# First FFN products by tiles of 128 tokens, in a fused sliding-window attention and SwiGLU kernel

## The chip, the cores and the metric

The kernel runs on one core of a Trainium2 chip. The time is device microseconds for one execution; eight runs of the kernel before had a median of 359.01 us (357.98 to 361.54). The profile comes from one execution, which took 359.05 us.

## What is computed

Attention over eight batches of 576 tokens, eight heads of 64, each token seeing itself and the 127 before it, with a bias by distance that differs by head. Its output, as 4608 tokens of 512, goes through a SwiGLU block:

```python
scores = scale * np.matmul(q, k.transpose(0, 1, 3, 2))
bias = slopes[:, None, None] * (-np.abs(rel).astype(np.float32))[None, :, :]
mask = (rel >= 0) & (rel < window)
scores = np.where(mask, scores + bias[None], -1000000000.0)
...
g = x @ w_gate
silu = g * (1.0 / (1.0 + np.exp(-g)))
val = x @ w_val
return (silu * val @ w_out).astype(np.float32)
```

The sizes of the block are 512 (model) and 1536 (hidden). Inputs and output are fp32; the kernel loads them converted to fp16.

## The kernel before

**Attention.** Batches are taken two at a time: four pairs (s), each with nine units (p), one for each tile of 128 query tokens (the ninth joins the last 64 tokens of both batches). A tile of 128 tokens of q, k or v is called by its rank, nine to a pair. For each unit, `scores` (line 226) multiplies k by q into score banks of PSUM (pool `ps_a`, tag "a", four banks, line 129); ACT takes the exponential (line 259), and DVE multiplies with the table that holds bias and mask (line 263). `weighted` (line 294) multiplies these weights with v, whose 65th column of ones gives the sums, and DVE divides (lines 316, 317). `x_transposed` (line 327) turns the result and ACT copies it to `xT` (line 341), the FFN's input. Each instruction at line 254 needs q and k transposed: up to rank 8 by PE (line 201, copy at 204 or 206), from rank 9 on by DMA transposes on SP's queue (line 222). The units up to FIRST = 4 use the gv banks (pool `ps_f`, three banks, line 128) for weighted sums; `REPEAT` (line 27) says how often PE makes a transpose at the start.

**FFN.** Nine blocks of 512 tokens. For each of twelve hidden slices m, `gate_val` (line 369) makes the gate product pg and the value product pv (line 363, `wide`, four matmuls each), ACT a tanh (374), DVE the gate sum uu (376) and the product hT (380). For block 0, `wide` may be called early for some of the columns; it keeps the bank in `early`, and a later call completes it. `OTHER` names the products that then use a score bank. Block 0's output projection is at line 393. The blocks from 1 to 7 use Strassen's scheme for the output projection: `sums` (line 443) makes sums of hT on DVE, and `strassen` (line 456) seven products of six matmuls (line 472) for each of two column tiles, with evacuations to ACT and DVE (lines 476 to 499) between. They are spread over the next block's half-steps (a gate or value product of one slice): `AT` (line 507) lists the half-steps after which one of the 14 products comes.

**Order.** Each engine works in program order. The first stage, `first_tiles` (line 566), and the first eight steps of the FFN are written out by hand for PE, DVE and ACT (`manual_schedule`, lines 659 to 667). After it, attention steps are drawn in at a rate that depends on the FFN step (lines 668 to 683), and a scheduler orders the instructions of each engine by a cost model when the kernel is built. Loads of q, k, v and weights are issued on POOL's queue (lines 168, 174, 609, 634); each waits until the transfer eight issues earlier has landed. A wait in a queue holds everything behind it. The first loads, up to w_out, are listed in lines 612 to 634.

Of the kernel before, what the change touches and what calls it, by code (L numbers as in the profile page):

```python
# [16 lines left out]
P = 128  # L17
# [6 lines left out]
ENGINES = {"all": None, "compute": {ET.PE, ET.DVE, ET.Activation}, "pe": {ET.PE}}  # L24
WARM = 7
IDLE = {("k", 0): 0, ("q", 0): 2}
REPEAT = {("q", 1): 4, ("k", 1): 4, ("q", 2): 3}
FIRST = 4
LEAD = 6
PRE = 0  # L30
# [4 lines left out]
def slot(h):  # L35

    return 4 * (h // 4) + 2 * (h % 2) + (h % 4) // 2
# [9 lines left out]
def kernel(  # L47
# [10 lines left out]
    nc = tc.nc  # L58
# [21 lines left out]
    idm = consts.tile([P, P], FP16, name="idm")  # L80
    nc.scalar.dma_start(idm, idm_d.ap())

    idm2 = consts.tile([P, P], FP16, name="idm2")
# [5 lines left out]
    def first_masks():  # L89
        nc.vector.tensor_copy(idf, idm)  # L90
        for h in sorted(range(H), key=slot):
            nc.scalar.activation(reg[:, slot(h), :], dist, AF.Exp, scale=-(2.0 ** (-8.0 * (h + 1) / H)))
# [5 lines left out]
    idle = kT[:, NK - 1].rearrange("p j t -> p (j t)")  # L98
# [66 lines left out]
    def load_v(rank):  # L165
        va[rank] = va_all[rank % NV]
        for (p0, p1), src in source(v, rank):
            nc.gpsimd.dma_start(va[rank][p0:p1, :, 0:D], src)  # L168
# [8 lines left out]
    def load(rank):  # L177
        load_qk(rank)
        load_v(rank)

    def transposed(name, rank):
# [16 lines left out]

        for _ in range(REPEAT.get((name, rank), 2) if rank < FIRST else 1):
            for j in range(4):  # L200
# [25 lines left out]
    def scores(i):  # L226

        s, p = units[i]
        def combined(n):
            return scores_128(s, (3, 7, 8)[n], 8, (s, "c", n), msk[n])  # L230

        def together(one, two):
            return [one[0] + two[0]] + one[1:] + two[1:]

        if p == 8:
            return together(combined(1), combined(2))
        if p == 7:
            return together(scores_128(s, p, p, (s, p), reg[:, :, 0:P]), combined(0))
        if p == 3:
            return scores_128(s, p, p, (s, p), reg[:, :, 0:P])  # L240
        ks = (9 * s + p) % NK
        banks = []
        e = epool.tile([P, H, 256], FP16, name="ex", tag="ex", bufs=4)
        ex[(s, p)] = e

        def products():
            for q4 in range(2):
                two = [ps_a.tile([P, 2, 256], FP32, name="ps", tag="a") for _ in range(2)]
                banks.append(two)
                for j in range(2):  # L250
                    pair = 2 * q4 + j
                    for par in range(2):
                        rows = slice(64 * par, 64 * par + 64)
                        nc.tensor.matmul(two[par][:, j, :], kT[rows, ks, pair, :],  # L254
                                         qT[rows, p:p + 2, pair, :], start=(j == 0), stop=(j == 1))

        def act(q4, par):
            o = 4 * q4 + 2 * par
            nc.scalar.activation(e[:, o:o + 2, :], banks[q4][par], AF.Exp, scale=scale)  # L259

        def mul(q4):
            o = slice(4 * q4, 4 * q4 + 4)
            nc.vector.tensor_mul(e[:, o, :], e[:, o, :], reg[:, o, :])  # L263

        return [[products], [lambda: act(0, 0)], [lambda: act(0, 1), lambda: mul(0)],
                [lambda: act(1, 0)], [lambda: act(1, 1), lambda: mul(1)]]
# [27 lines left out]
    def weighted(i):  # L294

        s, p = units[i]
        x = xpool.tile([P, H, D], FP16, name="x", tag="x")
        xs[i] = x
        for half in range(2):
            pool, tag = (ps_f, "gv") if i < FIRST else (ps_a, "a")  # L300
            av = pool.tile([P, 4, D + 1], FP32, name="av", tag=tag)
            todo = []
            for j in range(4):
                h = 4 * half + j
                if p == 8:
                    for n, kt in enumerate((3, 7, 8)):
                        todo.append((j, ex[(s, "c", n)][:, slot(h), :], va[9 * s + kt][:, h, :]))
                else:
                    if p not in (0, 4):
                        todo.append((j, ex[(s, p - 1)][:, slot(h), 128:256],  # L310
                                     va[9 * s + p - 1][:, h, :]))
                    todo.append((j, ex[(s, p)][:, slot(h), 0:128], va[9 * s + p][:, h, :]))
            for n, (j, w, val) in enumerate(todo):
                nc.tensor.matmul(av[:, j, :], w, val, start=(n == 0), stop=(n == len(todo) - 1))  # L314
            rec = xpool.tile([P, 4, 1], FP32, name="rec", tag="rec", bufs=4)
            nc.vector.reciprocal(rec, av[:, :, D:D + 1])
            nc.vector.tensor_mul(x[:, 4 * half:4 * half + 4, :], av[:, :, 0:D],  # L317
                                 rec.broadcast_to([P, 4, D]))
# [31 lines left out]
    hT = {}  # L350

    early = {}
    OTHER = {(0, 1, "v"), (0, 2, "g"), (0, 2, "v")}

    def wide(n, m, which, c1=512):

        w, ms = wg_sb if which == "g" else wv_sb, slice(m * P, (m + 1) * P)
        ps, c0 = early.pop((n, m, which), (None, 0))
        if ps is None:
            pool, tag = (ps_a, "a") if (n, m, which) in OTHER else (ps_f, "gv")  # L360
            ps = pool.tile([P, 512], FP32, name="p" + which, tag=tag)
        for kb in range(NKB):
            nc.tensor.matmul(ps[:, c0:c1], w[:, kb, ms], xT[n][:, kb, c0:c1],  # L363
                             start=(kb == 0 and c0 == 0), stop=(kb == NKB - 1 and c1 == 512))
        if c1 < 512:
            early[(n, m, which)] = (ps, c1)
        return ps
# [136 lines left out]

    AT = {*range(2, 9), *range(10, 17)}

    def ffn():

        for n in range(NBLK):
# [6 lines left out]
            for m in range(NMB):  # L518
                for half, _ in enumerate(gate_val(n, m)):
                    yield 1.0  # L520
                    if n > 1 and 2 * m + half in AT:
                        next(parts)
# [25 lines left out]
    def transposes_to(n):  # L548
        nonlocal done_t
        while done_t < n:  # L550
            transpose(done_t)
            done_t += 1
# [7 lines left out]
    def run(steps):  # L560
        for fs in steps:
            for f in fs:
                f()
            yield

    def first_tiles():

        first_masks()
        transposes_to(need[0] + 1)
        for n, _ in enumerate(run(scores(0))):  # L570
            if n == 2:
                transposes_to(need[1])
        for i in range(FIRST):
            if i + 1 < FIRST:
                for n, _ in enumerate(run(scores(i + 1))):
                    if n == 0 and i + 2 < FIRST:
                        transposes_to(need[i + 2])
            weighted(i)
            if i > 0:
                x_transposed(i - 1)  # L580

        for m, which in ((0, "g"), (0, "v"), (1, "g")):
            wide(0, m, which, 384)
        x_transposed(FIRST - 1)
        for m, which in ((1, "v"), (2, "g"), (2, "v")):
            wide(0, m, which, 384)

    def attention():

# [17 lines left out]
    def load_w(c0, c1):  # L607
        for src, dst in ((wg2, wg_sb), (wv2, wv_sb)):
            nc.gpsimd.dma_start(dst[:, :, c0:c1], src[:, :, c0:c1])
# [8 lines left out]
    load_qk(3, "k")  # L618
    load_v(2)
    load_v(3)  # L620
    load_w(0, 128)
    load_w(128, 512)
    load(4)
    load_qk(5, "q")
    load_w(512, 1024)
# [29 lines left out]
    def everything():  # L655
        nonlocal done
        base = 0
        busy(WARM)
        with tc.manual_schedule(engines=ENGINES[MANUAL]):
            first_tiles()  # L660
            done = FIRST
            steps = progress(ffn())
            while (at := next(steps)) < ALONE:
                if at == 4.0:
                    make_masks()
                if at == 6.0:
                    nc.scalar.copy(idm2, idm)
        for step in steps:

            b1 = 24 + 3 * PRE  # L670

            lead = LEAD if done < X_DMA_FROM - 2 else LEAD + 4
            blk = (0 if step + LEAD < b1 else 1 if step + LEAD < 60
                   else min(NBLK - 1, 2 + int((step + lead - 60) // 34.5)))
            if step < b1:

                target = base + max(0, step - ALONE) + max(0, step - 16) * (32 - b1 + ALONE) / (b1 - 16)
            elif step < 60:
                target = base + 32 + SECOND * 8 * (step - b1) / (60 - b1)
            else:  # L680
                target = base + 32 + SECOND * 8 + (step - 60) * RATE * 8 / 34.5
            while (n_att < target or done < ready[blk]) and att_step():
                pass

    everything()


# [28 lines left out]
```

## Time and profile before

| | |
|---|---|
| median of eight runs | 359.01 us |
| profiled execution | 359.05 us |
| its span, first to last instruction | 357.3 us |
| PE busy | 340.1 us, 95% |
| DVE busy | 271.0 us, 76% |
| DMA, 2 to 57 us | 169 to 181 GB/s |
| first FFN product starts | 21.43 us |
| first tanh starts | 25.97 us |
| first score of unit 9 starts | 60.67 us |
| projection of the last block starts | 343.24 us |

An idle time counts for the end only where the chain of work that ended last passes through it. The timeline gives for each instruction the idle time of its engine before it and what ended that time. The ends of matmuls are modelled, so a start is more reliable than an end.

### The profile page before, as it was taken

To read this page: it belongs to the slowest core of one execution; us is meant where nothing else is said; L and a number is where in the kernel's file an instruction comes from. 1 tells how busy PE (TensorE), PEld (TensorE's weight loads), DVE (VectorE), ACT (ScalarE), POOL (GpSimd) and SP (SyncE) were. 2 spreads that over 40 slices of the span, in tenths; PEclk is the share of its full clock that TensorE was granted. 3 is DMA by queue.
4 is the path that set the end of the run, shared out by engine and by line. 5 is a ranking of instruction groups with operands and counts; after the bars stand their busy time and mean duration, and the time that the engine had idled before them with its cause. 6 is when DMAs were issued, how large, how long until landed. Compare 5 with 4: busy or idle time off the path is not lost.

```text
span 357.3 us, 7133 instructions
## 1 busy us (share of the span) xinstructions
PE 340.1 (95%) x2701; PEld 193.8 (54%) x2701; DVE 271.0 (76%) x594; ACT 177.7 (50%) x351; POOL 107.0 (30%) x132
## 2 busy tenths in 40 slices
PE   7788997999999999999999999999999999999995
PEld 4554443444556645565466655564665566456543
DVE  4748974997987699768987998789877955975540
ACT  4837684455655455556565454555454323333321
POOL 8954652565827372844500001000000000000000
PEclk9999999999999999999999999999999999999999
DMA  9999999999999999999993213202021201101104
GB/s 151 172 186 186 167 175 99 141 134 149 161 142 147 154 155 185 178 153 163 171 106 89 42 65 32 87 18 75 15 76 29 75 4 57 60 2 60 60 17 103
DMA packets 159939, 37.87 MB, mean 106 GB/s; under 512 B 150432, under 2 KB 155424, under 8 KB 159904
## 3 DMA queue, kind: packets, MB, share of 16 engines
q0 software_dynamic: 116224, 18.62, 79.2%
q1 hardware_dynamic: 43232, 18.49, 28.5%
q8 instruction: 21, 0.34, 0.4%
q10 hardware_dynamic: 448, 0.30, 0.3%
q14 instruction: 14, 0.11, 0.1%
HBM read 37.91 MB, written 9.44 MB: 133 GB/s over the span
## 4 chain that ended last, share of the span: by engine, by line
PE 70%; DMA 12%; DVE 8%; POOL 4%; ACT 3%; issue 3%; ACTq 0%; POOLq 0%; SPq 0%; DVEq 0%
PE pg L363 21%; PE pv L363 21%; PE po L472 15%; DMA wv_sb<-in_moe_w_val_dram 6%; PE av L314 3%; PE ps L254 3%; DMA wo_sb<-in_moe_w_out_dram 3%; DMA qn<-in_q_dram 2%; PE po L393 2%; PE p L472 2%; DVE hT L380 2%; DVE uu L376 2%; POOL va L168 1%; ACT exc L286 1%; PE px L340 1%
## 5 line engine op out<-in xcount | busy, mean ns | idle before, releaser
L374 ACT ACTIVATE tt<-pg 128x512 f16<-128x512 f32 x108 | 64.8, 602 | 109.5 <-PE pg L363 103.5
L363 PE MATMUL pg<-xT,wg_sb 128*128 128x512 f16 (+2 forms) x444 | 115.4, 374 | 1.0 <-ACT xT L341 0.7
L363 PE MATMUL pv<-xT,wv_sb 128*128 128x512 f16 (+2 forms) x444 | 113.1, 373 | 1.2 <-DVE uu L376 1.2
L376 DVE SCALAR_TENSOR_TENSOR uu<-tt,pg 128x512 f16<-128x512 f16 x107 | 73.0, 683 | 37.9 <-ACT tt L374 37.3
L380 DVE TENSOR_TENSOR hT<-uu,pv 128x512 f16<-128x512 f16 x108 | 73.8, 683 | 6.0 <-PE pv L363 2.6
L363 PEld LDWEIGHTS <-wg_sb 128*128 128x128 f16 x444 | 41.6, 98 | 38.0 <-issue 3.5
L363 PEld LDWEIGHTS <-wv_sb 128*128 128x128 f16 x444 | 41.2, 98 | 38.5 <-issue 4.9
L259 ACT ACTIVATE ex<-ps 128x512 f16<-128x512 f32 x96 | 50.0, 608 | 9.7 <-PE ps L254 9.6
L168 POOL DMA_DIRECT2D va<-in_v_dram x40 | 34.2, 866 | 43.7 <-PE av L314 34.8
L174 POOL DMA_DIRECT2D qn<-in_q_dram x39 | 33.6, 866 | 35.7 <-DMA qT<-qn 18.4
L174 POOL DMA_DIRECT2D kn<-in_k_dram x39 | 33.3, 858 | 27.3 <-DMA kT<-kn 20.1
L472 PEld LDWEIGHTS <-hT 128*128 128x128 f16 x336 | 32.2, 98 | 14.9 <-issue 1.0
L263 DVE TENSOR_TENSOR ex<-ex,m_reg 128x1024 f16<-128x1024 f16 x48 | 32.8, 686 | 8.4 <-ACT ex L259 8.3
L472 PEld LDWEIGHTS <-S 128*128 128x128 f16 x252 | 23.9, 98 | 12.6 <-issue 4.1
L317 DVE TENSOR_TENSOR x<-av,rec 128x256 f16<-128x256 f32 x72 | 28.6, 420 | 0.4
L286 ACT ACTIVATE exc<-psc 128x512 f16<-128x512 f32 x40 | 21.0, 603 | 5.7 <-PE psc L282 5.7
L472 PE MATMUL po<-T,hT 128*128 128x256 f16 x168 | 22.9, 272 | 0.1
L472 PE MATMUL po<-T,S 128*128 128x256 f16 x168 | 22.9, 273 | 0.0
L314 PE MATMUL av<-va,ex 128*128 128x65 f16 x384 | 20.7, 193 | 2.2 <-DVE x L317 1.3
L314 PEld LDWEIGHTS <-ex 128*128 128x128 f16 x384 | 18.1, 97 | 6.3 <-DVE x L317 2.0
L254 PE MATMUL ps<-qT,kT 64*128 64x256 f16 x192 | 18.0, 272 | 3.6 <-DMA qT<-qn 2.0
L393 PE MATMUL po<-wo_sb,hT 128*128 128x512 f16 x84 | 19.7, 379 | 0.0
(72 smaller groups left out, 279.5 us busy)
## 6 DMA issues: line engine op xcount, KB each, us to landing
out_dram<-osb SPq DMA_DIRECT2D x32, 256.0 KB, 3.2
va<-in_v_dram POOLq DMA_DIRECT2D x32, 128.0 KB, 8.6
qn<-in_q_dram POOLq DMA_DIRECT2D x31, 128.0 KB, 7.4
kn<-in_k_dram POOLq DMA_DIRECT2D x31, 128.0 KB, 7.8
wo_sb<-in_moe_w_out_dram POOLq DMA_DIRECT2D x2, 768.0 KB, 9.6
wg_sb<-in_moe_w_gate_dram POOLq DMA_DIRECT2D x2, 512.0 KB, 10.6
wv_sb<-in_moe_w_val_dram POOLq DMA_DIRECT2D x2, 512.0 KB, 12.3
out_dram<-osb SPq DMA_DIRECT2D x6, 128.0 KB, 2.3
```

The lines of the kernel that those rows point to most:

```text
L168: nc.gpsimd.dma_start(va[rank][p0:p1, :, 0:D], src)
L174: nc.gpsimd.dma_start(t_[p0:p1], src)
L254: nc.tensor.matmul(two[par][:, j, :], kT[rows, ks, pair, :], qT[rows, p:p + 2, pair, :], start=(j == 0), stop=(j == 1))
L259: nc.scalar.activation(e[:, o:o + 2, :], banks[q4][par], AF.Exp, scale=scale)
L263: nc.vector.tensor_mul(e[:, o, :], e[:, o, :], reg[:, o, :])
L314: nc.tensor.matmul(av[:, j, :], w, val, start=(n == 0), stop=(n == len(todo) - 1))
L317: nc.vector.tensor_mul(x[:, 4 * half:4 * half + 4, :], av[:, :, 0:D], rec.broadcast_to([P, 4, D]))
L363: nc.tensor.matmul(ps[:, c0:c1], w[:, kb, ms], xT[n][:, kb, c0:c1], start=(kb == 0 and c0 == 0), stop=(kb == NKB - 1 and c1 == 512))
L374: nc.scalar.activation(tt, pg, AF.Tanh, scale=0.5)
L376: nc.vector.scalar_tensor_tensor(out=uu, in0=tt, scalar=one if (n, m) == PIN else 1.0, in1=pg, op0=ALU.add, op1=ALU.mult)
L380: nc.vector.tensor_mul(hT[n][:, m, :], uu, pv)
L472: nc.tensor.matmul(dst, a[:, m, cols], b[:, m, :], start=(start and m == 0), stop=(m == HM - 1), skip_group_check=True)
```

## The change

In the first stage, the products of block 0 for the slices m = 0 and 1 (gate and value) are begun as soon as the first tile of 128 tokens of xT is there, and continued tile by tile; those for m = 2 begin with two tiles. They were made for three tiles at once before, after the last of the weighted sums. The four products for m = 0 and 1 now lie in score banks. In the weighted sums of units 1 to 3, two products of zeros come first in each bank, which the real ones then overwrite. The counts of repeated transposes change, and q of rank 2 is transposed a little sooner. The first 512 columns of the gate and value weights are loaded as 256 and 256 instead of 128 and 384. The second copy of the identity is made at step 2 instead of 6, the masks at step 5 instead of 4. In the steps of the Strassen products, 4 and 10 are left out instead of 9, and 17 is added: from the third product of a block on, each comes half a step later.

```diff
-REPEAT = {("q", 1): 4, ("k", 1): 4, ("q", 2): 3}
+REPEAT = {("q", 1): 4, ("k", 1): 2, ("q", 2): 4}
...
             av = pool.tile([P, 4, D + 1], FP32, name="av", tag=tag)
+            if 0 < i < FIRST:
+
+                for _ in range(2):
+                    nc.tensor.matmul(av.rearrange("p j d -> p (j d)")[:, 0:256], idle[:, 0:P],
+                                     idle[:, 0:256], start=True, stop=True)
...
-    OTHER = {(0, 1, "v"), (0, 2, "g"), (0, 2, "v")}
+    OTHER = {(0, 0, "g"), (0, 0, "v"), (0, 1, "g"), (0, 1, "v")}
...
-    AT = {*range(2, 9), *range(10, 17)}
+    AT = {2, 3, *range(5, 10), *range(11, 18)}
...
+    def begin(n, tiles):
+
+        for m, which in ((0, "g"), (0, "v"), (1, "g"), (1, "v"), (2, "g"), (2, "v"))[:n]:
+            if early.get((0, m, which), (None, 0))[1] < tiles * P:
+                wide(0, m, which, tiles * P)
+
     def first_tiles():
 
         first_masks()
         transposes_to(need[0] + 1)
         for n, _ in enumerate(run(scores(0))):
-            if n == 2:
+            if n == 0:
                 transposes_to(need[1])
...
             weighted(i)
+
+            if i >= 2:
+                begin(4, i - 1)
             if i > 0:
                 x_transposed(i - 1)
-
-        for m, which in ((0, "g"), (0, "v"), (1, "g")):
-            wide(0, m, which, 384)
+        begin(6, 2)
+        begin(4, 3)
         x_transposed(FIRST - 1)
-        for m, which in ((1, "v"), (2, "g"), (2, "v")):
-            wide(0, m, which, 384)
+        begin(6, 3)
...
-    load_w(0, 128)
-    load_w(128, 512)
+    load_w(0, 256)
+    load_w(256, 512)
...
-                if at == 4.0:
+                if at == 2.0:
+                    nc.scalar.copy(idm2, idm)
+                if at == 5.0:
                     make_masks()
-                if at == 6.0:
-                    nc.scalar.copy(idm2, idm)
```

## The prediction

> **What bounds the kernel now.** I read the page first, then the chain that ended last in order of time, then the waits and the timeline of PE, then DMA by stretches. The page says that PE is the bound overall:
>
> ```profile
> span 357.3 us, 7133 instructions
> PE 340.1 (95%) x2701; PEld 193.8 (54%) x2701; DVE 271.0 (76%) x594; ACT 177.7 (50%) x351; POOL 107.0 (30%) x132
> PE 70%; DMA 12%; DVE 8%; POOL 4%; ACT 3%; issue 3%; ACTq 0%; POOLq 0%; SPq 0%; DVEq 0%
> ```
>
> 95% is an average over two regimes. The chain that ended last, in order of time, separates them (start, length, what):
>
> ```profile
> 12.34 8.00 DMA wv_sb<-in_moe_w_val_dram
> ...
> 22.55 13.07 DMA wv_sb<-in_moe_w_val_dram
> ...
> 36.84 9.43 DMA wo_sb<-in_moe_w_out_dram
> ...
> 47.43 8.74 DMA qn<-in_q_dram
> ...
> 56.25 4.29 DMA qT<-qn
> 60.54 0.14 issue
> 60.67 0.27 PE ps L254
> 60.94 0.97 PE pg L363 x4
> ```
>
> Up to 60.67 us no PE instruction is on the chain: it consists of loads, one handing over to the next on the POOL queue, then the transpose of q of rank 10 on SP's queue, which releases the first product of the first scores of batches 2 and 3 (unit 9). From there on it is PE nearly throughout. The change works before 27 us, inside the first regime. PE's timeline shows where it meets the loads (start, length, instruction, idle time before it and its releaser):
>
> ```profile
> 21.43 0.81 PE L363 MATMUL pg<-xT,wg_sb 128*128 128x384 f16 x4 [0.67 <-ACT xT L341]
> 37.56 0.40 PE L201 MATMUL pt<-idm,qn 128*128 128x128 f16 x4 [0.21 <-DMA qn<-in_q_dram]
> 60.67 0.27 PE L254 MATMUL ps<-qT,kT 64*128 64x256 f16 x1 [2.03 <-DMA qT<-qn]
> ```
>
> These are two gates. At 37.56 PE waits for the load of q of rank 6, issued at 24.57 and landed 13.0 us later, at 37.57. At 60.67 it waits for the rank-10 transpose. Are the loads limited by DMA, or by PE freeing buffers? By stretches (length, busy time of PE, PEld, DVE, ACT, POOL, then granted clock, DMA share, GB/s):
>
> ```profile
> 2.00:20.00 18.00, 13.94 (x175) 9.44 (x174) 11.55 (x37) 11.84 (x25) 17.08 (x21) 1.00 2.11 179
> 20.00:40.00 20.00, 17.72 (x140) 9.84 (x141) 13.26 (x25) 11.64 (x23) 11.35 (x15) 1.00 1.84 181
> 40.00:57.00 17.00, 15.93 (x169) 8.62 (x168) 14.39 (x35) 12.75 (x25) 8.19 (x10) 1.00 1.97 169
> 60.67:343.30 282.63, 279.72 (x2154) 159.47 (x2155) 228.47 (x493) 137.73 (x273) 68.90 (x83) 1.00 0.96 95
> ```
>
> DMA moves 169 to 181 GB/s from 2 to 57 us without a hole: in stretches of one microsecond, about 155 for q, k, v and 205 for weights, and only 40 to 41 us is lower (119). POOL's issues wait for the landing of the transfer eight issues earlier. So the time at which a load lands is a matter of the bytes ahead of it, not of PE. After 60.67, PE's idle time is 282.63 - 279.72 = 2.9 us: that is all that any later rearrangement could win.
>
> [...] the transposes that SP issued at 53.52, 54.87 and 56.25 land at 59.6, 60.1 and 60.5, when the loads issued on POOL up to 50 us have drained. [...] Here four 384-column products take 0.65 us and four 128-column ones 0.22, against 0.65 / 3 = 0.217. [...] The 2.03 us stall here leaves the clock at 1.00.
>
> **The change part by part.**
>
> *Transposes at the start.* k of rank 1 is transposed twice instead of four times: 8 fewer at 0.056 = 0.45 us. q of rank 2 four times instead of three: 4 x 0.056 = 0.22 more. Its copy (DVE, 0.42) now stands before both multiplications (0.69 each) of the first scores, instead of between them. Before, the copy ran at 11.24, behind a multiplication that had waited 1.01 us for ACT, and the second scores at 11.71 waited 1.24 us for it. The new order frees PE by some 1.0 us, of which the score banks that ACT still holds (its exponentials would end near 11.3) leave about 0.8.
>
> *Idle products.* 12 of 256 columns; six of that width start to start take 0.655 us (the groups of line 472), so 12 x 0.109 = 1.31 us. They lie between 12 and 21 us, where PE idles 0.41 + 0.26 + 0.77 + 0.28 + 0.16 + 0.67 = 2.55 us. If that cover were gone they would cost 1.31.
>
> *First products by tiles of 128.* Same columns (six products, four k-blocks, 512 columns each); 40 more instructions, at 0.22 per four no dearer. What moves is the time: 4 x 0.22 = 0.88 us of tile 0 ahead of the second x transpose, 0.88 of tile 1 ahead of the third. Together 1.76 us leave the run that now begins at 21.43, but filler and idle time compete for the same 2.55 us, and DVE, which runs without a hole from 12.9 to 21.5, sets when the last x comes. With the 0.8 from above I estimate that the six products end 1.5 us earlier than 26.9, and the first tanh (25.97 now) as much.
>
> *Banks.* Four of the six now sit in the four score banks, the pair of m=2 in two of three gv banks. The product of v for m=3 therefore waits for the third gate sum (two tanh-sum-product rounds later on DVE, 0.69 each); now it is at 28.20. DVE starts its queue of sums (idle 5.09 us until 26.60 now) 1.5 us earlier, so up to the first gate the head start stays about 1.5 us.
>
> *Weights in slices of 256 and 256.* Same bytes, same four issues. The four landed by 20.34 at 191 to 204 GB/s, later weights at 203 to 209, so at most 5% of the 0.5 MB in narrow slices, 0.13 us. I take 0.
>
> *Masks and second identity moved by a step.* 4 x 0.62 + 0.30 us of ACT, covered by its 2.30 us wait before 33.93. Without cover they would delay one tanh by up to 0.6. I take 0.
>
> *What the shift does to the queues.* In the program as built, POOL issues k and q of rank 8 ahead of both w_out halves instead of between them, and v of rank 9 ahead of k of rank 9. The set ahead of q of rank 10 is the same, so it lands at 56.2 again. k of rank 9 lands behind v: 54.3 becomes about 55.3 (one load of 128 KB in fp16 lands 0.7 to 1.2 us after another here). SP takes its transposes in order at 1.2 us each: 55.3 + 1.2 = 56.5 instead of 56.25 for rank 10. All end in one bunch behind the loads, so between 0 and 0.4 us later; I take +0.2.
>
> *Half a step later.* Seven blocks with two groups of seven products each; from the third product of a block on, each comes one half-step later. The waits of PE after 60 us:
>
> ```profile
> PE po L472 <- DVE osb L476: 1.2, 3, 0.4
> ```
>
> Three of 14 times the sixth product waits for the evacuation that follows the fifth, because a tanh and a gate sum (0.60 + 0.68) stand before it on DVE when the fifth comes after a gate product. The shift puts the fifth after a value product, and the seventh in the same position relative to the sixth's evacuation. Bounds: -1.2 if the waits vanish, 14 x 0.4 - 1.2 = +4.4 if every group gets one. I take 0, the waits changing place.
>
> *Sum.* PE passes the same work between the gates: leaving out filler, the same columns of products stand ahead of unit 9's scores in both programs. So the 1.5 us are waited out: 0.21 us of wait at 37.56 becomes about 1.7, and PE goes on at 37.57 as now. At unit 9 it arrives at 58.6 or, with DVE's backlog drained, up to 1 us earlier, and waits until 60.7 + 0.2. After that PE does what it does now. 357.3 + 0.2 = 357.5 of span, plus the 1.75 us by which the profiled execution (359.05) exceeds its span: 359.2. The median of the runs, 359.01, is within 0.04 of that execution.
>
> **Rivals.** *The head start reaches the end (faster).* For it, the gates must open earlier: q of rank 10 no longer waits in POOL's queue behind the landing of the first w_out half (46.28) and could be issued 1.4 us sooner, near 46.0. If it lands as much earlier, with all its transposes, unit 9 starts near 59.3; with the three waits gone too: 359.05 - 1.4 - 1.2 = 356.5; the first alone gives 357.6. Against it: DMA is full, and an earlier issue only stands longer in the queue.
>
> *Rank 9's k blocks SP (slower).* One mechanism: v ahead of k holds k's transpose, and rank 10's behind it in order. It decides (over 0.5%) once rank 10's transpose ends 1.8 us late, that is issued at 58.1, k landing at 56.9 or later, 2.6 us after now; one load costs about 1. At that point 360.9.
>
> *The half-step makes waits (slower).* At half of the 14 groups, 7 x 0.4 - 1.2 = +1.6: 360.7; at all of them 363.4. For it: the fifth-sixth pattern does return one product later. Against it: PE has other work between the two.
>
> *Half clock.* [...] I expect 2 to 3.
>
> **How the numbers follow.** Absorbed, 0.60, its own range 358.1 to 360.3. Head start reaches the end, 0.20. Rank 9's k on SP 0.06, half-step waits 0.10, half clock 0.04. A measurement of this kernel can tell about 0.5%, 1.8 us, from no change. Nearly all of the first case lies within it, as do small forms of the others: same 0.62, faster 0.20, slower 0.18. Leaving one in ten at each end, inside the faster case's 356.5 and the slower cases' 361 to 363, gives 357.0 to 361.3.
>
> **What would show it.** Right: first tanh near 24.5; the wait for the rank-6 q grown from 0.21 to 1 to 2 us with the product still at 37.5; unit 9's first score at 60.5 to 61.1 with a wait of 2 to 3.3 us; from there to the end 296.6 us as now. Wrong: unit 9 before 59.5 (loads not bytes-bound), or PE's idle time after it far from 2.9 us (the half-step), or first products not ahead of 26.9 (the banks or the filler).

## The result: slower by 0.8%, with the loss between 58 and 77 us

The kernel after has a median of 362.45 us (11 runs, 361.13 to 362.89) against 359.09 for the kernel before (32 runs). Over all runs the ratio is 1.0077, 95% interval 1.0059 to 1.0096; between the two medians it is 1.0094. The profiled execution took 362.92 us; the lines below are from it.

The head of the page (busy us, share of the span, instructions), and lines of the chain that ended last in order of time (start, length, what):

```profile
span 361.1 us, 7225 instructions
PE 343.8 (95%) x2749; PEld 196.9 (55%) x2749; DVE 272.5 (75%) x594; ACT 177.0 (49%) x351; POOL 106.9 (30%) x132
```

```profile
24.18 13.42 DMA qn<-in_q_dram
...
57.98 4.18 DMA qT<-qn
62.66 1.82 PE pg L368 x4
64.49 1.71 PE pv L368 x4
66.19 1.71 PE pg L368 x4
67.90 1.08 PE pv L368 x4
...
71.35 0.86 PE pg L368 x4
```

The chain has the same form: loads, then the transpose of q of rank 10, then PE. Two things differ. The transpose is issued at 57.98, not at 56.25, and the four products that follow unit 9's first score take 1.82, 1.71, 1.71 and 1.08 us. The last line, a product of the same shape, takes 0.86.

PE's timeline at the places that the prediction showed (start, length, instruction, idle time before it and its releaser):

```profile
24.52 0.38 PE L368 MATMUL pg<-xT,wg_sb 128*128 128x128 f16 x4 [0.23 <-ACT xT L346]
29.24 1.04 PE L368 MATMUL pv<-xT,wv_sb 128*128 128x512 f16 x4 [1.15 <-DVE uu L381]
37.65 0.40 PE L201 MATMUL pt<-idm,qn 128*128 128x128 f16 x4 [0.75 <-DMA qn<-in_q_dram]
62.30 0.37 PE L254 MATMUL ps<-qT,kT 64*128 64x256 f16 x1 [4.29 <-DMA qT<-qn]
77.42 0.61 PE L254 MATMUL ps<-qT,kT 64*128 64x256 f16 x8
```

And one line of the kernel before:

```profile
73.06 0.61 PE L254 MATMUL ps<-qT,kT 64*128 64x256 f16 x8
```

The first-stage edit does what it says. The last of the six products begins at 25.63 (before: 26.67), and the first tanh at 24.94 (before: 25.97): a head start of 1.0 us. PE then waits 1.15 us at 29.24. When it comes to the load of q of rank 6 it is about half a microsecond ahead (the transposes of k of that rank begin at 36.51 instead of 36.97), and it waits that out too: it goes on at 37.65 (before: 37.56). Between there and unit 9, three waits of 0.7 us in all that PE had for DVE in the kernel before are gone, and PE reaches unit 9 at 58.01 instead of 58.64. There it stands for 4.29 us instead of 2.03, and unit 9's first score is 1.63 us later than before (62.30 against 60.67). The last line of each is unit 10's scores.

By stretches of one microsecond (PE, PEld, DVE, ACT and POOL busy, then granted clock, DMA share, GB/s), the clock falls to half during that wait and stays there for some time behind it:

```profile
61.00:62.00 1.00, 0.00 (x0) 0.00 (x0) 0.00 (x0) 0.00 (x0) 0.19 (x1) 0.70 0.61 126
62.00:63.00 1.00, 0.70 (x2) 0.23 (x3) 0.00 (x0) 0.00 (x0) 1.00 (x2) 0.50 0.00 0
...
68.00:69.00 1.00, 1.00 (x5) 0.44 (x4) 0.43 (x1) 0.53 (x1) 0.00 (x0) 0.89 1.53 146
```

So the ledger of the two spans, 357.3 and 361.1, is: first score of unit 9, +1.63; from there to unit 10's scores, 15.12 us instead of 12.39, +2.73, the half clock; from unit 10's scores to the end, 283.68 instead of 284.24, -0.56. The sum is +3.80. The clock was down from about 61.4 to 68.2 us: in stretches of 0.2 us the profile has 0.50 in every one between these times and 0.96 to 1.00 beside them, so a mean of 0.70 in one microsecond is 0.4 us at full and 0.6 at half clock, and 0.89 is 0.22 at half and the rest at full. This profile, with a mean clock of 0.991, is no exception: of the twelve runs on record, this one included, eight had 0.990 or 0.991 and a median of 362.5 us, four had 0.994 or 0.995 and 361.3.

Why is the transpose late? SP's queue, before and after (start, length until the queue is free for the next):

```profile
53.52 1.30 SPq L222 DMA_TRANSPOSE qT<-qn  x1
54.87 1.25 SPq L222 DMA_TRANSPOSE kT<-kn  x1
56.25 8.88 SPq L222 DMA_TRANSPOSE qT<-qn  x2
```

```profile
53.92 1.31 SPq L222 DMA_TRANSPOSE qT<-qn  x1
55.85 1.45 SPq L222 DMA_TRANSPOSE kT<-kn  x1
57.98 8.51 SPq L222 DMA_TRANSPOSE qT<-qn  x2
```

Each of the three waits for its load, and q of rank 10, the last, landed at 57.9 instead of 56.2, although POOL issued it at 45.70 instead of 47.43. DMA moved less in between. Stretches of 5 us, before and after:

```profile
40.00:45.00 5.00, 4.83 (x38) 2.47 (x37) 4.71 (x12) 3.28 (x7) 3.55 (x5) 1.00 1.69 176
45.00:50.00 5.00, 4.84 (x52) 2.55 (x50) 3.67 (x10) 3.71 (x8) 3.70 (x5) 1.00 1.52 193
```

```profile
40.00:45.00 5.00, 5.00 (x39) 2.51 (x37) 4.75 (x12) 3.61 (x8) 4.05 (x6) 1.00 1.86 125
45.00:50.00 5.00, 4.84 (x58) 2.71 (x57) 4.56 (x11) 4.36 (x9) 4.24 (x5) 1.00 1.14 174
```

(51 + 19) x 5 = 350 KB fewer in ten microseconds; at the 185 GB/s that the kernel before held on average, 1.9 us. The delay of q of rank 10 is 1.7. What the queues carried from 40 to 43 us, before and then after:

```profile
DMA packets 713, 0.51 MB, mean 170 GB/s; under 512 B 245, under 2 KB 713, under 8 KB 713
```

```profile
DMA packets 2212, 0.32 MB, mean 106 GB/s; under 512 B 2188, under 2 KB 2210, under 8 KB 2210
```

Before, a half of w_out, in packets of 512 B to 2 KB (468 of the 713), runs alongside the small packets of rank 8. After, rank 8's six half-size loads (v, k, q, 64 partitions each) go ahead of both halves of w_out, and only small packets are there, moving 106 GB/s. The first theory therefore is: the change moved the order of the loads on POOL, the order cost 350 KB of transfer, q of rank 10 came 1.7 us later, and the longer wait brought the half clock (A). Rivals: the half-step of the sums; the order of v and k of rank 9; a loss behind 75 us.

### The profile page after: what moved, and what is told of

It reads as the page before. It is cut to its first block, busy times and chain, and to the rows that moved or that the text cites. A ratio compares the mean times of both kernels' runs of the same rounds, so it can differ in the third digit from the quotient of the medians.

```text
span 361.1 us, 7225 instructions
## 1 busy us (share of the span) xinstructions
PE 343.8 (95%) x2749; PEld 196.9 (55%) x2749; DVE 272.5 (75%) x594; ACT 177.0 (49%) x351; POOL 106.9 (30%) x132
## 4 chain that ended last, share of the span: by engine, by line
PE 75%; DMA 7%; DVE 6%; ACT 5%; POOL 4%; issue 2%; ACTq 0%; DVEq 0%; POOLq 0%
PE pg L368 22%; PE pv L368 22%; PE po L477 14%; PE po L398 4%; PE av L319 4%; DMA qn<-in_q_dram 4%; PE ps L254 3%; PE p L477 2%; DMA wv_sb<-in_moe_w_val_dram 2%; PE px L345 2%; ACT ex L259 2%; DVE hT L385 1%; DVE uu L381 1%; ACT exc L286 1%; POOL kn L174 1%
## 5 line engine op out<-in xcount | busy, mean ns | idle before, releaser
L368 PE MATMUL pg<-xT,wg_sb 128*128 128x512 f16 (+2 forms) x464 | 118.1, 369 | 0.2 <-ACT xT L346 0.2
L368 PE MATMUL pv<-xT,wv_sb 128*128 128x512 f16 (+2 forms) x464 | 115.7, 367 | 1.6 <-DVE uu L381 1.6
L368 PEld LDWEIGHTS <-wv_sb 128*128 128x128 f16 x464 | 43.1, 98 | 40.4 <-issue 5.2
L368 PEld LDWEIGHTS <-wg_sb 128*128 128x128 f16 x464 | 42.7, 98 | 35.9 <-issue 4.3
L346 ACT COPY xT<-px 128x512 f16<-128x512 f16 x24 | 14.1, 586 | 15.3 <-PE px L345 15.3
```

## Experiments

**w_out's first half ahead of k and q of rank 8**, as in the kernel before; v of rank 9 stays ahead of k.

```diff
-    load(8)
+    load_v(8)
+    nc.gpsimd.dma_start(wo_sb[:, 0:6, :], wo2[:, 0:6, :])
+    load_qk(8)
     loaded = 9
-    for a0 in (0, 6):
-        nc.gpsimd.dma_start(wo_sb[:, a0:a0 + 6, :], wo2[:, a0:a0 + 6, :])
+    nc.gpsimd.dma_start(wo_sb[:, 6:12, :], wo2[:, 6:12, :])
```

> The changed kernel with the first half of w_out issued ahead of k and q of rank 8 again, as in the kernel before; v of rank 9 stays ahead of k of rank 9. Theory A (six half-size loads in a row leave DMA underfed from 40 to 48 us, unit 9's gate comes late, and the longer idle time of PE drops its clock): DMA from 40 to 45 us goes from 125 back to 170 or more, q of rank 10 lands near 56.3 instead of 57.9, unit 9's first score starts at 60.6 to 61.0 with 2.6 to 3.2 us of wait, the clock stays at 1.00, and the time falls by 1.6 (gate) and 2.8 (clock) from 362.45 to about 358. Rival B (the first stage or the half-step itself costs the time): about 362. Rival C (v of rank 9 ahead of k of rank 9 is what makes the gate late): gate after 61.5, 361 to 362.

Measured: 359.05 us, ratio 0.9987 (0.9966 to 1.0008). The stretch from 40 to 45 us, SP's queue and the gate in its profile:

```profile
40.00:45.00 5.00, 5.00 (x39) 2.51 (x37) 4.74 (x12) 3.61 (x8) 3.62 (x5) 1.00 1.73 178
```

```profile
56.21 8.30 SPq L222 DMA_TRANSPOSE qT<-qn  x2
```

```profile
60.05 0.27 PE L254 MATMUL ps<-qT,kT 64*128 64x256 f16 x1 [2.04 <-DMA qT<-qn]
60.25 1.85 PE L368 MATMUL pg<-xT,wg_sb 128*128 128x512 f16 x4
61.89 1.91 PE L368 MATMUL pv<-xT,wv_sb 128*128 128x512 f16 x4
```

178 GB/s again, the transpose at 56.21, the gate at 60.05. The order of w_out and rank 8 explains the late gate; the order of rank 9's v and k costs nothing, since it is still changed here. The last two lines are a surprise: the clock is at half here too, after a wait of only 2.04 us (last section). The whole loss is gone with this one edit, although the head start is not won.

**The old steps of the sums in the kernel after.**

```diff
-    AT = {2, 3, *range(5, 10), *range(11, 18)}
+    AT = {*range(2, 9), *range(10, 17)}
```

> The changed kernel with the old half-steps for the Strassen products. Theory A: the first 70 us are the same, clock drop included, and the time is 362.0 to 363.0; the waits of PE for the evacuation after the fifth product come back (1.2 us), so rather the upper end. Rival B' (the half-step makes the change slower): 359 to 360.5.

Measured: 361.88 us, ratio 1.0060 (1.0039 to 1.0082); gate at 62.36, wait 4.41. The loss stays, so the half-step is not its cause.

**A product ahead of unit 9's scores, first attempt.** The scheduler puts one score of unit 9 ahead of five gate/value products and the other seven behind them. A useless product in its bank was to take this place, so that all eight scores come 4.3 us later and wait for nothing.

```diff
                 banks.append(two)
+                if i == 9 and q4 == 0:
+                    for _ in range(1):
+                        nc.tensor.matmul(two[0].rearrange("p a b -> p (a b)"), idle[:, 0:P], idle,
+                                         start=True, stop=True)
```

> The changed kernel with one product of zeros in front of unit 9's scores, in their own bank. The scheduler puts it where the first score was, and all eight scores behind the five gate and value products that follow (4.3 us of work). DMA is left as it is. Theory A: the transposes still come at about 62.2, but PE works until then; its wait falls from 4.29 to below 0.5 us, the clock stays at 1.00, and the time falls by 4.3 + 2.8 to about 355.5. Rival B: the wait was slack, about 362, or it moves to the next unit.

> The kernel before with the same product of zeros. Theory A: the wait of 2.03 us at 60.67 disappears, nothing else changes, 359.0 - 2.0 = 357.0. Rival (the wait is hidden by something else, or moves to unit 10): 358.5 to 359.5.

Measured: 375.31 (ratio 1.0412, 1.0337 to 1.0487) and 372.08 (1.0331, 1.0260 to 1.0403). The edit was at fault: the zeros lie in the kT tile that by then is the home of k of rank 11, so the product waited for that transpose, and PE with it, 18.24 us in the one and 11.81 in the other. They say nothing about the theories.

**The same with operands that were loaded long before**, in both kernels and with w_out's first half ahead.

```diff
+                if i == 9 and q4 == 0:
+                    for _ in range(1):
+                        nc.tensor.matmul(two[0].rearrange("p a b -> p (a b)"), idm, wg_sb[:, 0, 0:512],
+                                         start=True, stop=True)
```

> The kernel after, with one zero-cost product put in front of unit 9's scores: idm times the first 512 columns of the gate weights, into unit 9's own first score bank, which its scores then overwrite. It waits for no load. It takes the place that unit 9's first score had; the eight scores stand behind the five gate/value products (4.3 us of TensorE work) that stood behind the first. Theory A (the late transpose of q of rank 10 at 62.3 us, and the half clock after the 4.3 us wait, are the whole loss): TensorE starts the product near 58.0, reaches the scores at 58.0 + 0.2 + 4.3 = 62.5, no wait left, no half clock: 362.45 - 4.3 - 2.8 = 355.4 us, or up to 1 us more where waits come back later. Theory B (the first score's wait is waited out elsewhere anyway: ScalarE's exps or another transfer set the pace behind it): 360 to 362. Theory C (half of the loss lies behind 75 us): 357.5 to 359.

> The kernel before with the same product. Theory A: its wait of 2.03 us at unit 9's first score goes, and nothing else, since its clock was full there in the profile: 359.0 - 2.0 = 357.0 us (356.5 to 357.6). Then the kernel after with the product is 1 to 2 us faster than the kernel before with it, which is the head start of the first stage. Theory B: 358.5 to 359.

> The kernel after with the first half of w_out issued ahead of k and q of rank 8 (as in the kernel before) and with the same product. Theory A: the transpose of q of rank 10 is done near 60.05, and TensorE comes to the scores at 62.5, so it no longer waits: 355.4 us as with the product alone (355 to 356.5); the place of w_out is worth nothing more once nothing waits for the transpose. Rival: full DMA queues matter later as well, and this one is 1 us or more faster than with the product alone.

Measured: 361.89 us (ratio 1.0062, 1.0034 to 1.0091) where 355.4 was expected; 358.06 (0.9965, 0.9943 to 0.9986); 358.11 (0.9966, 0.9946 to 0.9986). The wait at unit 9 is gone in all three, as meant, but a wait at unit 10 has come in its place. The first, second and third of them:

```profile
75.36 1.04 PE L258 MATMUL ps<-qT,kT 64*128 64x256 f16 x8 [5.22 <-DMA kT<-kn]
```

```profile
72.19 0.61 PE L258 MATMUL ps<-qT,kT 64*128 64x256 f16 x8 [1.12 <-DMA kT<-kn]
```

```profile
73.06 1.03 PE L258 MATMUL ps<-qT,kT 64*128 64x256 f16 x8 [2.65 <-DMA kT<-kn]
```

Theory A in its first form falls: there is a second gate. It is the transpose of k of rank 10 (the expectations from here on call it rank 11 by mistake; the order of the transposes on SP's queue shows that it is 10). In the kernel before, PE came to unit 10 at 73.06 and the gate lay at 72.0 (issued at 65.50, landed 6.5 us later); the product could win 1 us and no more. In the kernel after, that transpose was issued at 67.89 and landed 5.1 us later, at 73.0, hidden behind the loss at unit 9. In the first of these runs it landed at 75.3, and DMA moved hardly anything (21 to 23 GB/s) between 69 and 71 us; no run here says why. POOL's queue in that run shows why k of rank 10 comes so late at all:

```profile
48.99 0.88 POOL L168 DMA_DIRECT2D va<-in_v_dram  x1 [0.59 <-DVE x L326]
61.80 0.87 POOL L174 DMA_DIRECT2D qn<-in_q_dram  x1 [11.94 <-DMA qT<-qn]
62.67 0.88 POOL L168 DMA_DIRECT2D va<-in_v_dram  x1
63.53 0.90 POOL L174 DMA_DIRECT2D kn<-in_k_dram  x1
```

POOL stands for 11.94 us until a transpose has read one of the four buffers that hold q as loaded, and k of rank 10 is issued behind that, at 63.53. So the two gates are coupled: what delays the rank-9 and rank-10 transposes delays the loads for unit 10 as well.

**Rank 8's halves first in the kernel before.** A fifth buffer lets POOL take the kernel after's order.

```diff
-    nat = ctx.enter_context(tc.tile_pool(name="nat", bufs=4))
+    nat = ctx.enter_context(tc.tile_pool(name="nat", bufs=5))
...
-    opool = ctx.enter_context(tc.tile_pool(name="op", bufs=8))
+    opool = ctx.enter_context(tc.tile_pool(name="op", bufs=7))
```

> The kernel before with a fifth buffer each for k and q as they are loaded (and seven instead of eight for the outputs on their way out, to make the room), which lets all six half-size loads of rank 8 be issued ahead of both halves of w_out, as in the kernel after; k of rank 10 then also goes ahead of q of rank 10, 0.8 us of transfer. Theory A (the order of rank 8's halves and w_out makes the late transpose): 110 to 130 GB/s between 40 and 45 us instead of 176, q of rank 10 at 58 to 59 us, its wait 4 to 5 us, half clock behind it: 363 to 365 us. Rival (the first-stage change or v of rank 9 ahead of k makes it): 170 to 180 GB/s, transpose 0.8 us later for k of rank 10, wait 2.8 us, 359.5 to 360.3.

Measured: 360.56 us, ratio 1.0035 (1.0004 to 1.0066). From 40 to 45 us:

```profile
40.00:45.00 5.00, 4.99 (x43) 2.61 (x41) 4.55 (x9) 4.22 (x9) 4.12 (x6) 1.00 1.75 122
```

The rate falls as theory A said, in a kernel without the first-stage change, and the transpose of q of rank 10 goes out at 58.23 instead of 56.25, though k of rank 10 now also goes ahead of it. The time does not follow: in this profile PE ran at half clock around 20 to 27 us (a mean of 0.58 from 20 to 25 and 0.74 from 25 to 30), came to unit 9 at 61.57 and waited for no transpose. With this order the rate was 122 GB/s instead of 176; for the time the run is inconclusive.

**The wait filled with work.** The kernel after with twenty of the useless product, one ahead of the five gate/value products and nineteen behind them.

```diff
+                if i == 9 and q4 == 0:
+                    for _ in range(20):
+                        nc.tensor.matmul(two[0].rearrange("p a b -> p (a b)"), idm, wg_sb[:, 0, 0:512],
+                                         start=True, stop=True)
```

> The kernel after with twenty of the same useless product (4.3 us of TensorE time) in the bank of unit 9's first score: one of them, the five gate/value products, the other nineteen, then unit 9's eight scores. TensorE works through where the kernel after waits 4.29 us, so nothing is won by the order but the clock. Theory A (the half clock behind the wait costs 2.8 us): it comes to unit 10's scores at 69.1 + 0.9 + 4.1 = 74.1 us instead of 77.4, no half clock near 60 to 80 us, 359.1 us; up to 360.5 where the transpose of k of rank 11 comes as late as 75.4, as in the run with one free product. Rival (what the half clock costs is waited out further on anyway): 362.0 to 362.8, as the kernel after.

Measured: 359.96 us, ratio 1.0029 (1.0012 to 1.0045). Lines of PE's timeline:

```profile
62.47 4.26 PE L252 MATMUL ps<-wg_sb,idm 128*128 128x512 f16 x19
66.66 0.61 PE L258 MATMUL ps<-qT,kT 64*128 64x256 f16 x8
...
74.57 0.61 PE L258 MATMUL ps<-qT,kT 64*128 64x256 f16 x8
```

PE is busy with nothing of use for as long as it stood still before, and the kernel is 2.5 us faster between the medians (362.45 - 359.96; by the two ratios 0.5%, 1.7 us), with a mean clock of 1.000 in this profile. Unit 10's scores come at 74.57 instead of 77.42. That is the price of the half clock.

**Both gates opened.** The fifth buffers, the single product, and both halves of w_out ahead of rank 8: in the kernel after, in the kernel before, and in the kernel after with the old steps of the sums.

```diff
+    for a0 in (0, 6):
+        nc.gpsimd.dma_start(wo_sb[:, a0:a0 + 6, :], wo2[:, a0:a0 + 6, :])
     load(8)
     loaded = 9
-    for a0 in (0, 6):
-        nc.gpsimd.dma_start(wo_sb[:, a0:a0 + 6, :], wo2[:, a0:a0 + 6, :])
```

> The kernel after with one free product at unit 9, both halves of w_out issued ahead of all of rank 8, and a fifth buffer each for k and q as loaded (outputs on their way out have seven buffers instead of eight). The loads of k of ranks 10 and 11 no longer wait for the transposes, so both gates come earlier: q of rank 10 before 61.6, k of rank 11 near 67 instead of 73 to 75. Theory A with the second gate (the loss is the two gates and the clock behind them, and nothing else): TensorE waits at neither, is at unit 9's scores at 62.5 and at unit 10's at 69.9: 362.45 - 7.5 = 355.0 us, 354.6 to 356. Rival (something behind 75 us, such as the half-step in the sums, holds the end): 357.5 or more with no wait at either gate.

> The kernel before with the same three edits. Theory A: it waits at neither gate and is at unit 9's scores at 63.2: 359.0 - 2.0 = 357.0 us. The kernel after with these edits is then 1.5 to 2 us faster: 0.7 to 1.2 us of first-stage head start, and up to 1 us of fewer waits for the buffers of the sums. Rival (the first-stage change brings nothing even without gates): both the same within 0.4 us.

> The kernel after with the three edits and with the old steps of the sums. With the old steps TensorE waited 1.2 us (three times 0.4) for the outputs' buffers, with the new ones 0.2. If those waits are on the path once the gates are open, this is 0.7 to 1.0 us slower than with the new steps; if they are waited out, the same within 0.4 us.

Measured: 357.76 (ratio 0.9960, 0.9946 to 0.9975), 358.00 (0.9957, 0.9937 to 0.9978) and 357.76 us (0.9957, 0.9942 to 0.9973). No gate is left in any, yet the first is 2.8 us above what was expected and hardly better than the kernel before with the same edits. It has new waits, for k and q of rank 8 behind 1.5 MB of w_out:

```profile
49.29 0.38 PE L201 MATMUL pt<-idm,kn 128*128 128x128 f16 x4 [1.14 <-DMA kn<-in_k_dram]
50.65 0.38 PE L201 MATMUL pt<-idm,qn 128*128 128x128 f16 x4 [0.43 <-DMA qn<-in_q_dram]
```

The old steps make no difference. They bring 1.5 us of waits for the outputs' buffers (0.2 with the new ones), but from unit 10's scores to the end both take 284.3 us: with the new steps PE waits 0.6 us for a sum that ACT copies and 0.4 for exponentials in the products of the output projection, waits that the old steps do not show.

**k and q of rank 8 between the two halves of w_out**, v of rank 8 last, with the fifth buffers and the single product, in both kernels; and the kernel after in its own order with only the fifth buffers and the product.

```diff
-    load(8)
+    for half in range(2):
+        nc.gpsimd.dma_start(wo_sb[:, 6 * half:6 * half + 6, :], wo2[:, 6 * half:6 * half + 6, :])
+        if half == 0:
+            load_qk(8)
+    load_v(8)
     loaded = 9
-    for a0 in (0, 6):
-        nc.gpsimd.dma_start(wo_sb[:, a0:a0 + 6, :], wo2[:, a0:a0 + 6, :])
```

> As the kernel after with the fifth buffers and the free product, but with the first half of w_out ahead of k and q of rank 8, its second half behind them and v of rank 8 last. With both halves ahead, TensorE waited 1.57 us for k and q of rank 8 at 49 to 51 us; these waits should go, and no wait at either gate come back: 357.76 - 1.6 = 356.2 us (355.7 to 356.8), unit 10's scores at 70.0. Rival (one more load is late behind these, so a head start is waited out at whichever load comes next): 357.3 or more, with a new wait for a load or a transpose.

> The kernel before with the same edits. It had no wait for a load between 20 and 75 us with both halves of w_out ahead, so nothing is won: 357.8 us (357.5 to 358.1). If e13 comes to 356.2, the difference of 1.6 us is the head start of the first stage that the change makes, and it reaches the end where no load gates it.

> The kernel after with its own order (all six half-size loads of rank 8 ahead of w_out), the fifth buffers and the free product. If the lower transfer rate between 40 and 45 us goes with the order, it stays at 100 to 130 GB/s here, and q of rank 10 is late (62 to 63 us), but TensorE comes to it at 62.5, and k of rank 11 comes before 70 since its load need not wait for a buffer: 355.5 to 357. Rival (the later k of rank 11 comes from the lost bytes and not from the buffer): k of rank 11 at 73 or later, a wait of 3 us or more at unit 10, 359 or more.

Measured: 356.34 us (ratio 0.9931, 0.9912 to 0.9950), 358.05 (0.9954, 0.9931 to 0.9977) and 356.44 (0.9932, 0.9910 to 0.9954). Unit 10's scores in the three:

```profile
69.94 0.61 PE L258 MATMUL ps<-qT,kT 64*128 64x256 f16 x8
```

```profile
71.20 0.61 PE L258 MATMUL ps<-qT,kT 64*128 64x256 f16 x8
```

```profile
70.43 0.61 PE L258 MATMUL ps<-qT,kT 64*128 64x256 f16 x8
```

With no load late, the head start reaches the end: 71.20 - 69.94 = 1.26 us between the two kernels in these profiles, 1.7 us between the medians. Not all of the 1.7 is the head start: among the runs with a mean clock of 0.998 or more, four of the kernel after with these edits and six of the kernel before, the medians are 356.34 and 356.95, 0.6 us apart, and the two groups do not overlap (356.01 to 356.51, 356.74 to 357.15). The other seven runs of the kernel before with these edits had 0.994 or 0.995 and a median of 358.12. The third is the change itself with one more buffer and one product. It still moves only 106 GB/s from 40 to 45 us:

```profile
40.00:45.00 5.00, 5.00 (x40) 2.62 (x39) 4.75 (x11) 3.61 (x8) 4.34 (x6) 1.00 1.44 106
```

and issues the transpose of q of rank 10 only at 59.48, but nothing waits for either. So the low rate by itself cost nothing in this run; in the kernel after it cost what it did because the first score of unit 9 stood ahead of 4.3 us of ready products, and because k of rank 10 could be loaded only behind a transpose. The buffer without the product was not run. Both versions beat both kernels, by 0.7% the kernel before.

## Why the prediction was wrong

Forecast were 359.2 us and a range up to 361.3; measured, 362.45. By its own steps:

- *Transposes at the start, idle products, first products by tiles.* Right in kind. The head start came to 1.0 us by the first tanh (24.94, where 24.5 was named) instead of the 1.5 estimated.
- *Banks.* Right: the value product of m=3 waits for the third gate sum, 1.15 us at 29.24, and goes on 1.0 us later than it did.
- *The first gate.* The place is right, PE goes on at 37.65; the wait is 0.75 us where 1 to 2 were named, since some half a microsecond of head start came that far and not 1.5.
- *What the shift does to the queues.* This is the step that failed. It saw the new order on POOL and concluded "the set ahead of q of rank 10 is the same, so it lands at 56.2 again", +0.2 at the gate. The set was the same, the rate was not. With the two rates that the prediction had read, 155 GB/s for q, k, v and 205 for weights, the order would not matter; but rank 8's halves with hardly any w_out beside them moved less than either, 79 to 140 between 40 and 43 us, and w_out alone then 166 to 187 until 48. In stretches of 5 us this is 125 and 174 GB/s instead of 176 and 193; so q of rank 10 came at 57.9 and the gate 1.63 later. The premise behind it, that the time of a landing is a matter of the bytes ahead, held only for the order in which it was measured. Putting w_out's first half back ahead of k and q of rank 8 gave 178 GB/s, the transpose at 56.21 and the gate at 60.05; the kernel before with rank 8's halves first gave 122 GB/s. (One reading was also too smooth: from 50 to 51 us the kernel before moved 143 GB/s, so 40 to 41 was not the only low microsecond.)
- *Rank 9's k blocks SP.* The transpose of rank 10 did come close to the 58.1 named there, but not for that reason: q of rank 10 had itself landed only then, and with w_out restored the same order of v and k left it at 56.21.
- *Half clock.* Named at 4 in 100, because the wait was put at 2 to 3 us; the price put on it was the author's estimate, which no trace had shown. The wait was 4.29 = 2.03 + 0.63 for coming earlier + 1.63 for the later gate. The price was 2.73 us in the trace, and 2.5 between the medians in the run that filled the wait: the clock stayed down for 6.8 us (61.4 to 68.2), and PE worked for 5.9 of them. It fell 3.4 us into the wait (58.01 to 61.4); with w_out's first half restored it fell behind a wait of 2.04 us, and in the kernel before it stayed at 1.00 behind one of 2.03. The head start itself lengthened the wait, by the 0.63 us that were left of it; whether a wait shorter by as much would have cost less no run shows.
- *Half a step later.* Taken as 0 with "the waits changing place": right, 357.76 us with either set of steps, and waits of PE for its sums in place of waits for the outputs' buffers.
- *After the gate.* "296.6 us from there to the end, as now" became 361.1 - 62.3 = 298.8: +2.73 for the clock, -0.56 for the rest. The idle time, 2.8 us, is as now; time lost to the clock counts as busy (PE 1.00 of every microsecond from 63 to 68 us).
- *The head start reaches the end.* Wrong for this kernel, right once no load is late. Not seen was the second gate at unit 10, which in the kernel before lay at 72.0, 1 us ahead of PE, and so would have held the gain to about 1 us even if the first had opened earlier.

## What to carry over

When a change reorders loads, count the transfer rate of the new order as unknown, above all where half-size loads are left to run alone: here it was 125 GB/s instead of 176 from 40 to 45 us, and behind the same bytes q of rank 10 landed at 57.9 instead of 56.2. A head start before a gate is not neutral: it lengthened the wait here by 0.63 us, and the half clock behind the wait of 4.29 cost another 2.73. Before forecasting what a gate absorbs, look for the next one: here opening one moved the wait to unit 10, then to rank 8, and the gain showed only when the third load was in time.

## What the hardware showed that was not expected

**Half clock behind a wait of 2.04 us.** With w_out's first half restored, PE stood for 2.04 us, 58.01 to 60.05, and right behind it the clock was at half for 3.4 us (0.66 + 1 + 1 + 0.74 of these stretches):

```profile
60.00:61.00 1.00, 0.95 (x3) 0.36 (x4) 0.00 (x0) 0.00 (x0) 1.00 (x2) 0.67 0.00 0
61.00:62.00 1.00, 1.00 (x4) 0.41 (x3) 0.00 (x0) 0.00 (x0) 1.00 (x2) 0.50 0.86 55
62.00:63.00 1.00, 1.00 (x4) 0.35 (x3) 0.23 (x1) 0.60 (x1) 1.00 (x2) 0.50 1.72 109
63.00:64.00 1.00, 1.00 (x4) 0.40 (x3) 0.67 (x2) 0.00 (x0) 1.00 (x3) 0.63 1.47 94
```

The kernel before waited 2.03 us at the same place and kept full clock in its profile. Of the 20 runs of that experiment, 11 had a mean clock of 0.994 or 0.995 and a median of 359.6 us, 9 had 0.999 or 1.000 and 358.6. Of the 182 runs of the kernel before that were made beside the experiments, only 71 had a mean clock of 0.998 or more: the profile at full clock stood for the smaller part of them. Their median, 358.8, is no lower than that of the 52 runs with 0.993 to 0.995, 358.7. In the profile of the kernel before with rank 8's halves first, the drop at 20 to 27 us fell ahead of the gate: PE came to unit 9 at 61.57 and waited for nothing there. What decides between the two clocks no run shows. The clock also fell without one long wait: in three of six profiles with the old first stage, PE ran at 0.58 to 0.66 of full clock from 20 to 25 us, after being busy only 3.3 to 3.4 of the 5 us before, with no single wait above 0.8 us there; the other three, busy for 3.2 to 3.3, kept full clock. All eleven profiles with the new first stage had a clock of 1.00 from 20 to 25 us; from 18.0 to 21.4 us PE is busy for 3.33 us in the kernel after and for 2.04 in the kernel before, whose profile also kept full clock. Some of what the change wins may lie there. In the interleaved pair 0.6 of the 1.7 us stand at full clock, so 1.1 go with the clock; that the seven runs lost it in the first stage is likely but not shown, since they were not profiled.

**The same bytes in another order.** In the kernel after, small loads alone moved 79 to 140 GB/s between 40 and 43 us, and w_out alone 166 to 187 until 48; mixed, in the kernel before, 162 to 206 from 41 to 46 us. But with both halves of w_out ahead of rank 8, w_out alone moved 202 to 212. The slow stretch is the one with rank 8's loads in halves, but halves that ran beside w_out were not slow (167 GB/s from 44 to 46 us in the kernel before). Small packets as such were not slow either: from 36 to 40 us, with whole tiles of rank 7 still on their way, the kernel after moved 154 GB/s, and 4832 of its 4833 packets were under 512 B. What was slow here is halves with little else beside them. Whether their shape does it, or that the eight transfers which POOL keeps on their way then hold fewer bytes, was not separated. (In the kernel before, the eighth issue behind w_out's first half stood for 1.30 us and went out at 46.56, that half having landed at 46.27.)
